# Cutting GpSimd's long elementwise operations into short ones in an attention-and-MoE kernel

## The chip, the core and the metric

The kernel runs on one core of one Trainium2 chip. The metric is the device time of one execution in microseconds (us). A core has several engines that run their own instruction streams and meet at semaphores: TensorE (PE, matmuls; its weight loads are listed as PEld), VectorE (DVE), ScalarE (ACT), GpSimd (POOL) and SyncE (SP), which here only issues DMAs. Each engine, and each DMA-issuing queue, takes its instructions in order, so an instruction that waits holds up all that stand behind it on the same engine.

## What is computed

For 8 batches, 8 heads, 576 rows and a head width of 64, a linear attention with two softmaxes is followed by a two-layer network with an exact GELU:

```python
q_s = softmax(q, over the head width)          # exp, then divided by the row's sum
k_s = softmax(k, over the sequence)
kv  = einsum('bhsd,bhse->bhde', k_s, v)        # one 64x64 matrix for each batch and head
att = einsum('bhsd,bhde->bhse', q_s, kv)       # 4608 tokens of width 512 = H*D
h   = att @ w_in                               # 512 -> 2048
out = gelu(h) @ w_out                          # 2048 -> 512, float32
```

The step that the change touches first is the division of `exp(q)` by its row sums: a multiplication of a 128x2048 bf16 tile by 32 reciprocals for each partition.

## The kernel before

The 4608 tokens are worked in chunks. Chunk c below 8 is the first 512 rows of batch c; chunk 8 collects the last 64 rows of all batches. For a chunk there are two phases: an `h` phase (`h_waves`, the first matrix product, GELU to the tile `g`) and a `y` phase (`y_phase`, the second product, into output tiles `y_sb`). Both products use Strassen-like schemes: seven block products for eight, with sums of blocks made on DVE, ACT and POOL. In the `y` phase of chunks 3 to 7 one of the seven products is itself cut a second time (class `Two`); its correction terms are put together on POOL (`corner`, `corner2`, `spread`).

While chunk c is in its `y` phase, the attention part of chunk c+1 is finished and that of batch `nb = c + 2` is begun. There is no planner: the order on every engine is written out by hand, and `after(i)` in `y_phase` runs a list of extra steps at a numbered point between the block products. For chunks 3 to 5 the steps that matter here stand in this order:

- At the head of the loop body for chunk c, `load(nb)` puts three DMAs on SP's queue: q (1 MB, line 112), k and v (1.15 MB each, line 130). On SP's queue they stand behind the two output stores of chunk c-1 (`y_store`, line 667), which end the previous `y_phase`.
- Point 8: `exp_q(nb)`, four exponentials on ACT (line 179) once q is there. Point 9: `exp_k(nb)` on ACT (line 184).
- Point 0, on POOL: `touch_g` (line 1201, a one-column operation that waits for DVE's last sum on `g`), `corner`, then the first of four casts of v to bf16 (`cast_v`, line 196). Then `corner2`, and at point 6 the other three casts.
- Point 1: `norm_q(nb)`: DVE sums the rows of `exp(q)` and takes reciprocals (lines 269 and 270), then POOL scales the tile `eq` (named `e` in the profile) in one operation of 2048 columns (line 275).
- After the fourth block product, `spread` and two additions on POOL into the output block `c22`, a 2x256 column view of a `y_sb` tile: `c22 += c12`, then `c22 -= c21` (lines 838 and 839, recorded under the helper's line 434).
- Point 5, `next_x`: on PE the attention product of chunk c+1 (line 349); on SP the DMA transpose of the scaled `eq` (line 329), which is needed one chunk later; on PE `kv_step(nb)` (line 231), 72 small matmuls of `exp(k)` with the cast v, in two halves, the first over casts 0 and 1 and the second over casts 2 and 3. On DVE stand between them `x_sums` (line 458 through the helper at 434), differences of `xT` blocks into `quad_t`, and the division of kv by its sums (lines 251 and 252).
- Then PE runs the last block product (7), and SP issues `y_store(c, 1)`, which holds `c22`, and `y_store(c, 0)`.

For c = 6 the load is `load_qrest`, eight DMAs of the remaining q rows, in place of `load(nb)`. For chunks 7 and 8 nothing is loaded. Chunk 1 also has the two additions into `c22`, with `load(4)` behind its stores.

Of the kernel before, what the change touches and what calls it, by code (L numbers as in the profile page):

```python
# [11 lines left out]
ALU = mybir.AluOpType  # L12
# [4 lines left out]
def kernel(  # L17
# [16 lines left out]
    nc = tc.nc  # L34
    B, H, S, D = q.shape
    NT, DM = out.shape
    DF = moe_w_in.shape[1]
    J = 4
# [27 lines left out]
    def bank(i, name="ps", shape=(128, 512)):  # L66
        return psum.tile(list(shape), FP32, tag=f"k{i}", name=name)
# [21 lines left out]
    HN = DM // 2  # L89
# [10 lines left out]
    def table(func):  # L100
        nc.scalar.activation(out=scr[:, 1:2], in_=scr[:, 0:1], func=func)

    st = [dict() for _ in range(B + 1)]
# [42 lines left out]
    def load(b):  # L146
        load_main(b, "q", q)
        load_pair(b, "k", k)
        load_pair(b, "v", v)

    def load_qrest():
        f = f32in.tile([128, 2048], FP32, tag="qf")
        f = f.rearrange("p (j h d) -> p j h d", j=J, h=H)
        st[B]["qf"] = f
        for b in range(B):
            nc.sync.dma_start(
                out=f[(b % 2) * R:(b % 2 + 1) * R, b // 2, :, :],
                in_=q[b, :, M:S, :].rearrange("h p d -> p h d"),
            )
# [21 lines left out]
    def exp_k(b, parts=1, part=None):  # L181
        n = HP // parts
        for i in range(0, HP, n) if part is None else (part * n,):
            nc.scalar.activation(  # L184
                out=ek[b % 2][:, i:i + n],
                in_=st[b]["kf"][:, i:i + n].rearrange("p x (n d) -> p x n d", n=NS),
                func=AF.Exp,
            )
# [75 lines left out]
    def q_sums(b, i=0, n=1):  # L264

        w = H // n
        qsum = small.tile([128, J, w], FP32, tag="qsum")
        st[b]["recq"] = small.tile([128, J, w], FP32, tag="recq", name="recq")
        nc.vector.reduce_sum(out=qsum, in_=st[b]["eq"][:, :, i * w:(i + 1) * w, :], axis=AX.X)  # L269
        nc.vector.reciprocal(st[b]["recq"], qsum)  # L270

    def q_scale(b, eng, i=0, n=1):
        w = H // n
        e = st[b]["eq"][:, :, i * w:(i + 1) * w, :]
        eng.tensor_tensor(  # L275
            out=e, in0=e, in1=st[b]["recq"].unsqueeze(3).to_broadcast([128, J, w, D]), op=ALU.mult,
        )

    def norm_q(b, i=0, n=1, eng=None):

        q_sums(b, i, n)
        q_scale(b, eng or nc.gpsimd, i, n)
# [108 lines left out]
    def s_parts(c, p0, n, which):  # L391


        g = st[c]["g"]
        a, b = slice(p0, p0 + n), slice(p0 + HK, p0 + HK + n)
        lo, hi = slice(0, HT), slice(HT, M)
        tt = nc.vector.tensor_tensor
        if 0 in which:
            tt(out=s5[:, a], in0=g[:, a, lo], in1=g[:, b, lo], op=ALU.add)
        if 1 in which:  # L400
            tt(
                out=s12[:, a].rearrange("p k (u m) -> p k u m", u=2),
                in0=g[:, a].rearrange("p k (u m) -> p k u m", u=2),
                in1=g[:, b, hi].unsqueeze(2).to_broadcast([128, n, 2, HT]), op=ALU.add,
            )
        for i, half in ((3, lo), (4, hi)):
            if i in which:
                tt(out=s12[:, a, half], in0=g[:, a, half], in1=g[:, b, hi], op=ALU.add)  # L408
        if 2 in which:
            tt(out=g[:, a, hi], in0=g[:, a, hi], in1=g[:, a, lo], op=ALU.subtract)  # L410
            tt(out=g[:, b, lo], in0=g[:, b, lo], in1=g[:, b, hi], op=ALU.subtract)  # L411
# [21 lines left out]
    def tt(out, in0, in1, op=ALU.add, eng=nc.vector):  # L433
        eng.tensor_tensor(out=out, in0=in0, in1=in1, op=op)  # L434
# [229 lines left out]
    def y_store(c, half, y_sb):  # L664
        j = 2 * half
        dst = out[c * S:c * S + M, :].rearrange("(p j) n -> p j n", j=J)[:, j:j + 2, :]
        nc.sync.dma_start(out=dst, in_=y_sb)
# [4 lines left out]
    def y_operands(c):  # L672
        g = st[c]["g"]
        act = {
            1: s12[:, :, LO], 2: s12[:, :, HI], 3: g[:, UP, LO], 4: g[:, DN, HI],
            5: s5, 6: g[:, UP, HI], 7: g[:, DN, LO],
        }
        wgt = {
            1: w16[:, 0], 2: wo_bf[:, UP, 0:HN], 3: wo_bf[:, UP, HN:DM],
            4: wo_bf[:, DN, 0:HN], 5: wo_bf[:, DN, HN:DM], 6: w16[:, 1], 7: w7,  # L680
        }
        return act, wgt
# [85 lines left out]
    def y_phase(c, ins, p3=None):  # L768

        act, wgt = y_operands(c)
        if c == 1:
            at = {"bd": 3, "be": 4, "bb": 0, "bx": 1, "ba": 2}
        else:
            at = {"bd": roles["x0"], "be": roles["x1"], "bb": roles["bb"], "bx": roles["x2"], "ba": roles["ba"]}
        bd, be, bb, bx, ba = (bank(at[n], "y" + n[1]) for n in ("bd", "be", "bb", "bx", "ba"))
        ysb = [moe_sb.tile([128, 2, DM], FP32, tag="y_sb", name="y_sb", bufs=2) for i in range(2)]
        c11, c12 = ysb[0][:, :, 0:HN], ysb[0][:, :, HN:DM]
        c21, c22 = ysb[1][:, :, 0:HN], ysb[1][:, :, HN:DM]  # L780
        f = zeros32

        def two(ps):
            return ps.rearrange("p (j n) -> p j n", j=2)

        def mm(m, ps, first):
            for j in range(2):
                for k in range(HK):
                    nc.tensor.matmul(  # L789
                        ps[:, j * HN:(j + 1) * HN], act[m][:, k, j * 128:(j + 1) * 128],  # L790
                        wgt[m][:, k, :], start=(first and k == 0 and j == 0),
                        stop=(k == HK - 1), skip_group_check=True,
                    )

        def after(i):
            for fn in ins.get(i, []):
                fn()

        if p3:
            p3.mm(c, bx, (4, 5, 1), True)  # L800
            p3.snap(bx)
        mm(4, bd, True)
        if c > 1:
            nc.scalar.copy(out=f, in_=bd)
            after(8)
            if p3:
                p3.mm(c, bx, (2, 3, 6, 7), False)
            else:
                mm(3, bx, True)
            nc.scalar.copy(out=c12, in_=two(bx))  # L810
            after(9)
        else:
            nc.vector.tensor_copy(out=f, in_=bd)
        after(0)
        if p3:
            p3.corner2(c12)
        after(6)
        mm(5, be, True)
        after(7)
        tt(f, f, be, ALU.subtract)  # L820
        after(1)
        if c > 1:
            tt(c12, c12, two(be))
        mm(1, ba, True)
        tt(c22, two(f), two(ba))
        after(2)
        mm(2, bd, False)
        nc.scalar.copy(out=c21, in_=two(bd))
        after(3)
        if c == 1:  # L830
            mm(3, be, False)
            nc.scalar.copy(out=c12, in_=two(be))
        after(10)
        mm(6, bb, True)
        tt(c22, c22, two(bb))
        if p3:
            p3.spread(c12)
        tt(c22, c22, c12, eng=nc.gpsimd)
        tt(c22, c22, c21, ALU.subtract, eng=nc.gpsimd)
        after(5)  # L840
        mm(7, ba, False)
        tt(c11, two(f), two(ba))
        y_store(c, 1, ysb[1])
        y_store(c, 0, ysb[0])
        after(4)
# [328 lines left out]
    def first_weights():  # L1174
        nonlocal y3
        y3 = Two()
        y3.weights(0)

    y_phase(1, {
        0: [sums[3]],  # L1180
        7: [lambda: norm_q(2, 0, 2)],
# [16 lines left out]
    def touch_g(c):  # L1198


        nc.gpsimd.tensor_copy(out=scr[:, 2:3], in_=st[c]["g"][:, NDF - 1, 0:1])  # L1201
# [12 lines left out]
    for c in range(2, B + 1):  # L1214
        nb = c + 2
        if 2 < c and nb < B:
            load(nb)
        elif nb == B:
            load_qrest()
        p3 = y3 if 2 < c < B else None  # L1220
        h_waves(c, q_late if c == 2 else None, p3 and p3.sums)
        s_parts(c, 4, 4, (2,))
        yi = {}
        if nb <= B:
            yi[8] = [lambda: exp_q(nb)]
            yi[1] = [lambda: norm_q(nb)]
            yi[3] = [lambda: table(AF.Gelu)]
        if nb < B:
            yi[9] = [lambda: exp_k(nb)]
            cv = [lambda hp=hp: cast_v(nb, hp, nc.gpsimd) for hp in range(HP)]  # L1230
            yi[0] = [lambda: touch_g(c)] + ([p3.corner] if p3 else []) + cv[:1]
            yi[6] = cv[1:]
        elif p3:
            yi[0] = [p3.corner]
        if c < B:
            yi[5] = [lambda: next_x(c, nb)]
            y_phase(c, yi, p3)
        else:
            y_last(c)
# [30 lines left out]
```

## Time and profile before

| what | value |
|---|---|
| median of three runs | 258.1 us (257.6 to 258.83) |
| the profiled execution: its own time | 257.78 us |
| the profiled execution: span of the trace | 255.7 us |
| PE busy | 248.8 us (97%) |
| DVE busy | 221.5 us (87%) |
| ACT busy | 190.9 us (75%) |
| POOL busy | 89.8 us (35%), 100 instructions |
| granted clock of TensorE | 1.00 |

The page lists busy time by engine, then groups of instructions by source line, with the operands by the program's names, the shape (partitions x columns) and how often they ran. In the lists in order of time, the first column is the start in us from the start of the span, the second the duration; a bracket at the end gives idle time of the engine ahead of the instruction and what ended it. "x4" after a shape means that four such instructions in a row are told as one line.

### The profile page before, as it was taken

What the parts mean: (1) busy time and instruction counts of PE and PEld (TensorE: products, weight loads), DVE (VectorE), ACT (ScalarE), POOL (GpSimd) and SP (SyncE); (2) the same over time, 40 slices, a digit from 0 to 9 for tenths busy, and PEclk for the clock granted to TensorE, in tenths of its full rate; (3) what the DMA queues carried; (4) which work ended last, traced back from release to release, by engine and by line L of the source; (5) the groups of instructions that cost most, each with busy time, mean ns of one, the idle gap of its engine ahead of it and who ended that gap; (6) DMA issues with size and microseconds to landing.
All of it is one profiled execution on the core that took longest, in us unless ns stands there. A gap on an engine that the chain in (4) does not pass through costs nothing.

```text
span 255.7 us, 6732 instructions
## 1 busy us (share of the span) xinstructions
PE 248.8 (97%) x2732; PEld 195.7 (77%) x2738; DVE 221.5 (87%) x395; ACT 190.9 (75%) x326; POOL 89.8 (35%) x100
## 2 busy tenths in 40 slices
PE   7999999999999999999999999999999999999994
PEld 3444444448888889898889878987899889988883
DVE  1878799888986999998999899989999999878972
ACT  4785988699977995889588968896787778258711
POOL 1530023001949377007900691059203920540000
PEclk9999999999999999999999999999999999999999
DMA  7999999994549925980379137922760250013033
GB/s 241 400 368 425 401 406 399 399 411 171 75 145 326 276 47 145 328 315 1 85 252 402 49 71 231 385 98 47 224 146 3 46 200 2 3 44 124 0 82 85
DMA packets 43167, 50.23 MB, mean 196 GB/s; under 512 B 20225, under 2 KB 30465, under 8 KB 42881
## 3 DMA queue, kind: packets, MB, share of 16 engines
q1 hardware_dynamic: 42416, 49.13, 56.6%
q10 hardware_dynamic: 720, 0.69, 1.1%
q8 instruction: 21, 0.34, 0.5%
q14 instruction: 10, 0.07, 0.1%
HBM read 36.70 MB, written 9.44 MB: 180 GB/s over the span
## 4 chain that ended last, share of the span: by engine, by line
PE 83%; DVE 6%; DMA 4%; ACT 2%; issue 2%; ACTq 0%; POOL 0%; DVEq 0%
PE qa L503 19%; PE ps L383 11%; PE qb L503 10%; PE yd L789 8%; PE ya L789 7%; PE ps L648 5%; PE qc L503 4%; PE ye L789 4%; PE yb L789 3%; PE yx L743 2%; DMA f<-in_v_dram 2%; DMA touch<-in_moe_w_in_dram 2%; DVE qsum L269 2%; DVE y_sb L434 2%; PE kv L231 1%
## 5 line engine op out<-in xcount | busy, mean ns | idle before, releaser
L503 PEld LDWEIGHTS <-quad_s 128*128 128x128 bf16 x448 | 43.4, 98 | 7.7 <-DVE kvc L252 1.1
L275 POOL TENSOR_TENSOR e<-e,recq 128x2048 bf16<-128x2048 bf16 (+1 forms) x9 | 27.4, 3046 | 49.7 <-DVE recq L270 49.1
L789 PEld LDWEIGHTS <-g 128*128 128x128 bf16 x368 | 35.2, 98 | 4.8 <-issue 0.4
L503 PEld LDWEIGHTS <-wi_bf 128*128 128x128 bf16 x336 | 32.8, 98 | 3.9
L789 PEld LDWEIGHTS <-s 128*128 128x128 bf16 x336 | 32.7, 98 | 3.7
L503 PE MATMUL qa<-quad_t,quad_s 128*128 128x256 bf16 x224 | 29.8, 272 | 0.2 <-DVE qb L434 0.2
L383 PE MATMUL ps<-xT,wi_bf 128*128 128x512 bf16 x124 | 27.8, 379 | 0.3
L269 DVE TENSOR_REDUCE qsum<-e 128x16 f32<-128x1024 bf16 (+1 forms) x12 | 20.9, 1745 | 6.8 <-ACT e L179 6.6
L383 PEld LDWEIGHTS <-wi_bf 128*128 128x128 bf16 x128 | 12.4, 98 | 15.2 <-issue 0.6
L527 ACT ACTIVATE g<-r 128x512 bf16<-128x512 f32 x28 | 17.3, 631 | 7.3 <-DVE r L434 7.3
L511 ACT COPY qc<-qa 128x512 f32<-128x512 f32 x26 | 13.9, 577 | 11.4 <-PE qa L503 5.6
L389 ACT ACTIVATE g<-ps 128x512 bf16<-128x512 f32 x32 | 17.6, 603 | 6.2 <-PE ps L383 5.8
L434 DVE TENSOR_TENSOR qb<-qa,r 128x512 f32<-128x512 f32 x28 | 18.1, 691 | 4.6 <-ACT g L527 2.9
L179 ACT ACTIVATE e<-f 128x512 bf16<-128x512 f32 (+1 forms) x42 | 20.5, 556 | 2.0 <-DMA f<-in_q_dram 1.8
L527 ACT ACTIVATE g<-qc 128x512 bf16<-128x512 f32 x28 | 15.2, 594 | 8.2 <-PE qc L503 8.2
L434 POOL TENSOR_TENSOR y_sb<-y_sb 128x512 f32<-128x512 f32 x14 | 18.9, 1351 | 3.7 <-issue 2.8
L408 DVE TENSOR_TENSOR s<-g 128x1024 bf16<-128x1024 bf16 x28 | 19.8, 726 | 0.0
L196 POOL CAST v_aug<-f 128x576 bf16<-128x576 f32 x25 | 17.4, 723 | 3.7 <-DMA f<-in_v_dram 3.5
L434 DVE TENSOR_TENSOR r<-qa,r 128x512 f32<-128x512 f32 x28 | 17.9, 680 | 0.8 <-PE qa L503 0.7
L1201 POOL CAST scr<-g 128x1 f32<-128x1 bf16 x4 | 0.7, 187 | 49.5 <-DVE g L411 49.5
L184 ACT ACTIVATE ek<-f 128x2304 bf16<-128x2304 f32 (+1 forms) x10 | 17.4, 1735 | 0.5 <-DMA f<-in_k_dram 0.5
L503 PE MATMUL qb<-quad_t,quad_s 128*128 128x256 bf16 x112 | 15.6, 273 | 0.3 <-DVE kvc L252 0.2
(116 smaller groups left out, 536.7 us busy)
## 6 DMA issues: line engine op xcount, KB each, us to landing
out_dram<-y_sb SPq DMA_DIRECT2D x16, 512.0 KB, 4.3
f<-in_k_dram SPq DMA_DIRECT2D x6, 1152.0 KB, 9.9
f<-in_v_dram SPq DMA_DIRECT2D x6, 1152.0 KB, 11.6
f<-in_q_dram SPq DMA_DIRECT2D x6, 1024.0 KB, 8.2
w<-in_moe_w_in_dram SPq DMA_DIRECT2D x6, 512.0 KB, 9.1
f<-in_v_dram SPq DMA_DIRECT2D x8, 288.0 KB, 6.3
f<-in_q_dram SPq DMA_DIRECT2D x4, 512.0 KB, 8.9
w<-in_moe_w_out_dram SPq DMA_DIRECT2D x2, 1024.0 KB, 12.3
```

The lines of the kernel that those rows point to most:

```text
L179: nc.scalar.activation(out=dst[:, i], in_=src[:, u], func=AF.Exp)
L184: nc.scalar.activation(out=ek[b % 2][:, i:i + n], in_=st[b]["kf"][:, i:i + n].rearrange("p x (n d) -> p x n d", n=NS), func=AF.Exp,)
L196: eng.tensor_copy(out=o, in_=i)
L269: nc.vector.reduce_sum(out=qsum, in_=st[b]["eq"][:, :, i * w:(i + 1) * w, :], axis=AX.X)
L275: eng.tensor_tensor(out=e, in0=e, in1=st[b]["recq"].unsqueeze(3).to_broadcast([128, J, w, D]), op=ALU.mult,)
L383: nc.tensor.matmul(ps, wi_bf[:, dm, t * 128:(t + 1) * 128], st[c]["xT"][:, dm, :], start=(dm == 0), stop=(dm == NDM - 1),)
L389: nc.scalar.activation(out=st[c]["g"][:, t, :], in_=ps, func=AF.Gelu)
L408: tt(out=s12[:, a, half], in0=g[:, a, half], in1=g[:, b, hi], op=ALU.add)
L434: eng.tensor_tensor(out=out, in0=in0, in1=in1, op=op)
L503: nc.tensor.matmul(held[kind, q][:, u], w, mov[m][:, k], start=(m in (1, 5) and u == 0 and k == 0), stop=(k == 1), skip_group_check=True,)
L527: nc.scalar.activation(out=g[:, t:t + 2, half], in_=held[kind, q], func=AF.Gelu)
L789: nc.tensor.matmul(ps[:, j * HN:(j + 1) * HN], act[m][:, k, j * 128:(j + 1) * 128], wgt[m][:, k, :], start=(first and k == 0 and j == 0), ...
```

## The change

The scaling of `eq` by POOL at point 1, in chunks 2 to 6, becomes eight operations of 256 columns, each over four heads of one of the four row groups. The row sums and reciprocals on DVE stay one operation each. The scalings of batches 0 to 3 stay as they are.

The two additions into `c22`, in all of chunks 1 to 7, become eight operations of 128 columns: first the four parts of `c22 += c12`, then the four parts of `c22 -= c21`. The arithmetic on each element is the same.

```diff
+    def q_scale_parts(b):
+
+        for j in range(J):
+            for i in (0, 4):
+                e = st[b]["eq"][:, j, i:i + 4, :]
+                nc.gpsimd.tensor_tensor(
+                    out=e, in0=e, op=ALU.mult,
+                    in1=st[b]["recq"][:, j, i:i + 4].unsqueeze(2).to_broadcast([128, 4, D]),
+                )
...
         if p3:
             p3.spread(c12)
-        tt(c22, c22, c12, eng=nc.gpsimd)
-        tt(c22, c22, c21, ALU.subtract, eng=nc.gpsimd)
+        for x, op in ((c12, ALU.add), (c21, ALU.subtract)):
+            for j in range(2):
+                for n in (slice(0, 128), slice(128, HN)):
+                    tt(c22[:, j, n], c22[:, j, n], x[:, j, n], op, eng=nc.gpsimd)
         after(5)
...
             yi[8] = [lambda: exp_q(nb)]
-            yi[1] = [lambda: norm_q(nb)]
+            yi[1] = [lambda: q_sums(nb), lambda: q_scale_parts(nb)]
             yi[3] = [lambda: table(AF.Gelu)]
```

## The prediction

> **What bounds the kernel now.** I read the page first, then the chain of work that ended last, then each engine's list in order of time around one `y` phase (chunk 4, 137 to 160 us), and last the DMA issues with their time to landing.
>
> The page, with the groups that the change touches:
>
> ```profile
> PE 248.8 (97%) x2732; PEld 195.7 (77%) x2738; DVE 221.5 (87%) x395; ACT 190.9 (75%) x326; POOL 89.8 (35%) x100
> ...
> L275 POOL TENSOR_TENSOR e<-e,recq 128x2048 bf16<-128x2048 bf16 (+1 forms) x9 | 27.4, 3046 | 49.7 <-DVE recq L270 49.1
> ...
> L434 POOL TENSOR_TENSOR y_sb<-y_sb 128x512 f32<-128x512 f32 x14 | 18.9, 1351 | 3.7 <-issue 2.8
> ```
>
> PE is the bound on the whole, and POOL seems to have two thirds of the span to spare. But the average hides a tight ring. POOL's list for chunk 4:
>
> ```profile
> 142.43 0.19 POOL L1201 CAST scr<-g 128x1 f32<-128x1 bf16 x1 [14.06 <-DVE g L411]
> 142.57 0.99 POOL L434 TENSOR_TENSOR two_d<-two_d 128x128 f32<-128x128 f32 x2
> 143.59 0.66 POOL L196 CAST v_aug<-f 128x576 bf16<-128x576 f32 x1
> 144.21 0.99 POOL L434 TENSOR_TENSOR two_d<-two_d,y_sb 128x128 f32<-128x128 f32 x2
> 145.15 1.88 POOL L196 CAST v_aug<-f 128x576 bf16<-128x576 f32 x3
> 146.99 3.62 POOL L275 TENSOR_TENSOR e<-e,recq 128x2048 bf16<-128x2048 bf16 x1
> 150.57 1.05 POOL L434 TENSOR_TENSOR y_sb<-y_sb,two_d 128x128 f32<-128x128 f32 x2
> 151.69 2.88 POOL L434 TENSOR_TENSOR y_sb<-y_sb 128x512 f32<-128x512 f32 x2
> ```
>
> From 142.43 to 154.57 POOL has no gap. What it ends with releases SP's queue, here for chunks 3 and 4:
>
> ```profile
> 128.39 0.84 SPq L667 DMA_DIRECT2D out_dram<-y_sb  x2
> ...
> 132.13 0.66 SPq L130 DMA_DIRECT2D f<-in_v_dram  x1
> ...
> 154.60 0.84 SPq L667 DMA_DIRECT2D out_dram<-y_sb  x2
> ...
> 157.87 0.73 SPq L130 DMA_DIRECT2D f<-in_v_dram  x1
> ```
>
> The store goes out 0.03 us after POOL's last addition (151.69 + 2.88 = 154.57), and the next batch's q, k and v stand behind it. The issues between 129 and 134 us, with time to landing in the last column:
>
> ```profile
> f<-in_v_dram SPq DMA_DIRECT2D x1, 1152.0 KB, 11.3
> ```
>
> So v lands at 132.13 + 11.3 = 143.4, and POOL's first cast of it starts at 143.59, just behind `corner` (142.57 + 0.99 = 143.56). Here v arrives just when it is wanted. For chunk 5 it lands at 157.87 + 11.5 = 169.4, and the cast starts at 169.71. The casts end at 147.03, and PE asks for them soon after:
>
> ```profile
> 147.66 0.81 PE L231 MATMUL kv<-v_aug,ek 64*64 64x65 bf16 x72
> ```
>
> Its second half, at about 148.0, needs the last two casts: 0.95 us to spare. The ring is v landing, casts, scaling, additions, store, loads, v landing: 143.4 to 169.4, 26.0 us, while PE takes 150.16 - 124.25 = 25.9 and 26.2 us for these two chunks. POOL is thus almost a second bound in chunks 3 to 5.
>
> The other thing to see is a DVE operation on the chain:
>
> ```profile
> 149.24 1.65 DVE quad_t L434
> ...
> 151.35 1.05 PE qb L503 x8
> ```
>
> This difference of two SBUF blocks takes 0.41 us elsewhere. Here it ends at 150.89, 0.28 after POOL's scaling ended at 150.61. In chunks 3 and 5 it is the same (1.56 and 1.57 us, ending 0.29 and 0.28 after the scaling). DVE is shut out until POOL's long operation is over, and PE's next product starts late.
>
> **What the change takes away.** DVE's wait shrinks from up to the rest of a 3.62 us operation to at most the rest of a short one. Its worth on PE is read from PE's starts, where eight such matmuls take 0.87 us: the product behind starts 0.19, 0.32 and 0.25 us late in chunks 3, 4, 5, the one that waits on `e_sum` behind the third `quad_t` another 0.13, 0.12, 0.12, and 0.37 in chunk 6; chunks 2 and 7 lose nothing. That is 1.5 us at most. [...]
>
> **What it adds on POOL.** The scaling took 3.62 us for 2048 columns and 1.90 for 1024, so 0.185 us is fixed and a part of 256 columns costs 0.185 + 0.43 = 0.61. Independent POOL operations overlap a little (three casts of 0.66 take 1.88, a spacing of 0.61), so eight parts take 7 x 0.57 + 0.61 = 4.6 us: +1.0. For the additions the nearest row is exact in shape: 128x128 float32 takes 0.455 alone. At a spacing of 0.41 eight take 3.3, at the 0.50 of the pair `two_d` (dependent, 0.99 for two) 4.0; two long ones take 2.62 where DVE leaves them alone (chunk 1). I take 3.4, nearer the independent spacing, since each subtraction depends on an addition four places ahead: +0.8. [...]
>
> Each DVE operation that now gets in holds POOL: the first `spread` operation took 0.63 against 0.455, the first addition 1.46 against 1.27, so 0.2 each. In the scaling that is one or two `quad_t` differences, and since POOL runs later into the next chunk, the fourth one and the three sums of `Two.sums` (156.09 to 157.0) meet it too: 3 to 5 more, +0.7. Together POOL ends 2.5 us later in a chunk. Low end 1.5 (0.9, 0.6, nothing for DVE), high end 3.6 (1.3, 1.3, 1.0).
>
> **What waits behind it.** SP's transpose waits for the last part, 1.3 us or more later; its result is wanted 25 us later, nothing. The stores and loads move by the full 2.5.
> - Chunk 1: only the additions, +0.8; v for chunk 2 lands at 77.11 + 12.2 = 89.3, wanted at 90.96. Hidden. Chunk 7's store has no load behind it, nothing.
> - Chunk 2: about +2.2 (no `spread`); v lands at 103.75 + 11.3 = 115.05, wanted at 117.39. Just hidden; without that cover it would add to all that follows.
> - Chunk 3's lateness meets chunk 4: v late by 2.5, less 0.95: kv, and PE behind it, 1.55 us late.
> - Chunk 4's ring starts from that late v and adds 2.5: 2 x 2.5 less 0.95 less the 0.3 by which v was early: PE 3.7 us late against before.
> - Chunk 5 adds 2.5 again; behind its store stand the eight loads of the remaining q. The last is issued at 187.6 and lands 3.2 later at 190.8; its exponential starts at 193.63, 2.8 to spare. From it DVE's row sums run without a gap to the last `xT` copy, ready 0.2 before PE's product at 201.85. So 3 x 2.5 - 0.3 - 2.8 - 0.2 = 4.2 us late, which includes the 3.7.
> Lateness counted from a landing swallows what PE gained ahead of it, so of the 1.5 only chunk 6's 0.3 is left: +3.9.
>
> The q and k loads are covered: in chunk 4 q lands at 129.28 + 8.4 = 137.7 for 141.30, k at 140.6 for 143.87.
>
> **Sum.** The profiled execution took 257.78 us (span 255.7, 2.1 around it), 0.3 under the median of 258.1. 257.8 + 3.9 = 261.7, and 262.0 on the median's scale. With 1.5 us a chunk, chunk 5 decides: 2 x 1.5 - 1.25 - 0.3 = +1.4, 259.5; with 3.6: 10.8 - 3.3 - 0.3 = +7.2, 265.3.
>
> **Rivals.**
> - The relief wins (faster). The place is the first `quad_t` difference behind the attention product, the price 1.5 us on PE, less what is left of a short wait (0.3 us of some 1.2): 257.0. It needs POOL's added time to stay below about 0.85 us a chunk, since 2 x 0.85 - 1.25 - 0.3 is near zero. For it: the wait stands on the chain three times. Against it: 14 more instructions with a fixed 0.185 less 0.05 overlap make 1.8 already. [...] Chance 0.10.
> - The lateness is hidden: v is there earlier than the landing time says, or the ring has a microsecond more in it. Then only the relief and DVE's new short waits are left, and they cancel: 258.1. Against it: the cast of chunk 4 starts 0.03 after its forerunner, where unhindered casts start 0.04 before its end. Chance 0.08.
> - Worse than the ring: short POOL operations shut DVE out again and again (14 openings of 0.2 to 0.5 us in DVE's fullest stretch), and the lateness of chunk 2 joins in. By the ring 4 x 2.5 - 2.3 - 3.3 = +4.4, and half a microsecond of DVE's lateness in each of four chunks adds 2: +6.4, 264.5 and more. Chance 0.10.
>
> **How the numbers follow.** My forecast has 0.72. The measurement tells about 0.5% (1.3 us) from no change. Slower is the forecast and the worse case, 0.72 + 0.10 = 0.82; same 0.08; faster 0.10. The range from 259.0 to 265.5 runs from the low cost, half a microsecond under it for a partial relief, to the high cost; it leaves out the relief, the hidden case and the far end of the worst.
>
> **What would show it.** POOL's scaling as eight of about 0.6 us spanning 4.6 to 5.2, the additions as eight of 0.45 to 0.6 spanning 3.3 to 4.2; the first `quad_t` difference down from 1.6 to 0.5 to 1.0 us; the stores of chunk 3 at about 131 and of chunk 4 some 5 later than before; POOL idle ahead of line 196 until `f<-in_v_dram`; PE waiting ahead of line 231 for `v_aug` in chunks 4 and 5, and the exponential of chunk 6 waiting for `f<-in_q_dram`. I am wrong if the store of chunk 3 moves by less than 1 us, or if casts wait for v and PE does not wait for casts.

## The result, and the profile after

The changed kernel is slower: 261.42 us median (261.02 to 262.39) against 258.17, a ratio of 1.013 (95% interval 1.009 to 1.017). A second series on another occasion gave 261.85 against 257.85, 1.015 (1.014 to 1.017). The profiled execution took 261.10 us with a span of 259.0.

The page after, first the totals, then the two groups of the change (the added function moves line 434 to 444):

```profile
PE 250.9 (97%) x2738; PEld 197.5 (76%) x2738; DVE 219.3 (85%) x395; ACT 190.8 (74%) x326; POOL 103.5 (40%) x177
...
L444 POOL TENSOR_TENSOR y_sb<-y_sb 128x128 f32<-128x128 f32 x56 | 26.1, 500 | 2.8 <-issue 2.8
L284 POOL TENSOR_TENSOR e<-e,recq 128x256 bf16<-128x256 bf16 x40 | 24.9, 657 | 1.8 <-DVE recq L270 1.2
```

DVE's busy time fell by 2.2 us, as it waits less inside its operations (the mean of `quad_t<-xT` is 579 ns and was 951). POOL's rose by 13.7. That POOL is busy for 40% of the span and idle for the rest says nothing about the loss. POOL's list in order of time around chunk 4, and the first cast of chunk 5, does:

```profile
145.42 0.66 POOL L196 CAST v_aug<-f 128x576 bf16<-128x576 f32 x1 [2.30 <-DMA f<-in_v_dram]
146.04 0.98 POOL L444 TENSOR_TENSOR two_d<-two_d,y_sb 128x128 f32<-128x128 f32 x2
146.97 1.88 POOL L196 CAST v_aug<-f 128x576 bf16<-128x576 f32 x3
148.82 5.15 POOL L284 TENSOR_TENSOR e<-e,recq 128x256 bf16<-128x256 bf16 x8
153.93 0.86 POOL L444 TENSOR_TENSOR y_sb<-y_sb,two_d 128x128 f32<-128x128 f32 x2
154.76 4.01 POOL L444 TENSOR_TENSOR y_sb<-y_sb 128x128 f32<-128x128 f32 x8
...
173.37 0.66 POOL L196 CAST v_aug<-f 128x576 bf16<-128x576 f32 x1 [3.17 <-DMA f<-in_v_dram]
```

The scaling takes 5.15 us in place of 3.62, the additions 4.01 in place of 2.88. POOL now stands idle for 2.30 and 3.17 us ahead of the first cast because v is not there; before, it had no gap at that place. The reason stands on SP's queue, chunks 3 and 4:

```profile
130.51 0.83 SPq L677 DMA_DIRECT2D out_dram<-y_sb  x2
...
133.78 0.79 SPq L130 DMA_DIRECT2D f<-in_v_dram  x1
...
158.79 0.83 SPq L677 DMA_DIRECT2D out_dram<-y_sb  x2
...
162.05 0.83 SPq L130 DMA_DIRECT2D f<-in_v_dram  x1
```

The store of chunk 3 goes out 2.12 us later than before (130.51 against 128.39), that of chunk 4 4.19 later (158.79 against 154.60): the lateness adds up around the ring. The chain of work that ended last shows how it reaches PE in chunk 4:

```profile
133.78 11.52 DMA f<-in_v_dram
...
146.04 0.45 POOL two_d L444
...
147.06 0.70 DVE y_sb L444
...
147.80 0.67 PE ps L359 x7
148.47 0.40 DVE y_sb L444
...
148.91 0.47 PE kv L231 x34
```

In the chain of before, this stretch was PE's matmuls up to 139 us and then ACT and DVE work, with no DMA in it. Now it is the transfer of v, `corner2` on POOL (which stands behind the first cast), DVE's addition into `c12` (which has to wait for `corner2` to have read it: DVE idles 1.40 us until then), PE's attention product (one of its output banks is the one that this addition empties: PE idles 0.64 us until then), and the second half of kv.

What held that second half back is not the DVE row that the chain names. DVE's list has it as

```profile
148.45 0.69 DVE L444 TENSOR_TENSOR y_sb<-y_sb,yb 128x512 f32<-128x512 f32 x1
```

and so running on to 149.14, while the second half starts at 148.91. What had just ended is POOL's last cast (146.97 + 1.88 = 148.85), and in the trace the matmul at 148.91 waits on the semaphore that POOL's casts raise. So two branches lead from the late v to PE: a first wait through `corner2` and DVE, and behind it a last one for the casts. The product behind kv waits for both, and it is the last that counts.

### The profile page after: what moved, and what is told of

The parts are those of the page before. It is cut to its first block, busy times and chain, and to the rows that moved or that the text cites. A ratio compares the mean times of both kernels' runs of the same rounds, so it can differ in the third digit from the quotient of the medians.

```text
span 259.0 us, 6822 instructions
## 1 busy us (share of the span) xinstructions
PE 250.9 (97%) x2738; PEld 197.5 (76%) x2738; DVE 219.3 (85%) x395; ACT 190.8 (74%) x326; POOL 103.5 (40%) x177
## 4 chain that ended last, share of the span: by engine, by line
PE 77%; DMA 13%; DVE 4%; SPq 2%; issue 2%; POOL 1%; POOLq 0%; DVEq 0%
PE qa L513 15%; DMA f<-in_v_dram 11%; PE ps L393 11%; PE ya L799 9%; PE qb L513 7%; PE yd L799 7%; PE ps L658 5%; PE ye L799 4%; PE qc L513 4%; PE yb L799 3%; PE kv L231 2%; PE yx L753 2%; PE ps L359 2%; DMA f<-in_q_dram 2%; PE ya L882 1%
## 5 line engine op out<-in xcount | busy, mean ns | idle before, releaser
L799 PEld LDWEIGHTS <-g 128*128 128x128 bf16 x368 | 36.0, 100 | 5.5 <-issue 0.4
L513 PE MATMUL qa<-quad_t,quad_s 128*128 128x256 bf16 x224 | 29.2, 273 | 0.0
L275 POOL TENSOR_TENSOR e<-e,recq 128x1024 bf16<-128x1024 bf16 (+1 forms) x4 | 9.3, 2330 | 48.1 <-DVE recq L270 48.1
L444 POOL TENSOR_TENSOR y_sb<-y_sb 128x128 f32<-128x128 f32 x56 | 26.1, 500 | 2.8 <-issue 2.8
L284 POOL TENSOR_TENSOR e<-e,recq 128x256 bf16<-128x256 bf16 x40 | 24.9, 657 | 1.8 <-DVE recq L270 1.2
```

The lines of the kernel that those rows point to most:

```text
L284: nc.gpsimd.tensor_tensor(out=e, in0=e, op=ALU.mult, in1=st[b]["recq"][:, j, i:i + 4].unsqueeze(2).to_broadcast([128, 4, D]),)
L513: nc.tensor.matmul(held[kind, q][:, u], w, mov[m][:, k], start=(m in (1, 5) and u == 0 and k == 0), stop=(k == 1), skip_group_check=True,)
L799: nc.tensor.matmul(ps[:, j * HN:(j + 1) * HN], act[m][:, k, j * 128:(j + 1) * 128], wgt[m][:, k, :], start=(first and k == 0 and j == 0), ...
```

## The experiments

**The changed kernel once more** (no edit).

> The changed kernel once more, for a second trace. It is to show whether the stretch of product 7 in chunk 5 that took 3.50 us instead of 1.75 for sixteen matmuls (granted clock 0.97 over that chunk) belongs to the change or to that one execution. Ring theory (POOL's added 2 us a chunk delay the stores, the loads behind them, the casts of v and PE): 261 to 262 us with or without the slow stretch, and POOL idle ahead of the first cast of v by 1.5 to 2.5 us in chunk 4 and by 2.5 to 4 in chunk 5. Rival (the throttled clock makes up half of the loss): an execution at clock 1.00 takes 259.5 us or less.

Measured: 261.85 us, ratio 1.015 (1.014 to 1.017). The trace is of an execution at clock 1.00, and its product 7 in chunk 5 takes the usual 1.75 us; yet its time is that of the series. POOL waits 2.95 us (above the 1.5 to 2.5 that I gave) and 3.20 us for v. What it loses in place of the slow stretch shows in ACT's list for chunk 6, where the exponential's table load waits for the last of the remaining q rows:

```profile
196.86 1.28 ACT L179 ACT_TABLE_LOAD   x1 [1.42 <-DMA f<-in_q_dram]
```

The other executions say the same: six of the nine of the changed kernel have a mean clock of 0.993, about what one such stretch makes (3.41 us at 0.50 in a span of 259.0), and none of the 17 of the kernel before in the second series is under 0.998. Those six average 261.7 us, the three at 1.00 average 261.5. So the throttled stretch is not what costs the time; the rival falls. A lateness that is counted from a landing swallows a loss on PE ahead of it, as it swallows a gain.

**Each half alone.** In the first kernel the additions are whole again:

```diff
-        for x, op in ((c12, ALU.add), (c21, ALU.subtract)):
-            for j in range(2):
-                for n in (slice(0, 128), slice(128, HN)):
-                    tt(c22[:, j, n], c22[:, j, n], x[:, j, n], op, eng=nc.gpsimd)
+        tt(c22, c22, c12, eng=nc.gpsimd)
+        tt(c22, c22, c21, ALU.subtract, eng=nc.gpsimd)
```

> The scaling in eight parts, the additions whole. Ring theory: POOL ends 1.2 to 1.4 us later a chunk (the scaling spans 4.8 to 5.0 us against 3.62), which the 0.95 us of chunk 4 and the 1.25 us of chunks 4 and 5 together mostly cover; PE is late by 0.3 in chunk 4 and 1.2 in chunk 5, less 0.5 to 0.8 of relief: 258.0 to 259.3 us. Rival (short POOL operations as such disturb DVE, in proportion to their number, 40 of the 96 new ones): about 0.4 of the whole loss, 259.5 us.

Measured: 259.36 us (258.39 to 260.25), ratio 1.006 (1.004 to 1.008), just above the range of the ring and nearer to the rival's 259.5. POOL waits 1.85 us for v in chunk 4 and 1.81 in chunk 5.

In the second the scaling is whole and the additions are split:

```diff
-            yi[1] = [lambda: q_sums(nb), lambda: q_scale_parts(nb)]
+            yi[1] = [lambda: norm_q(nb)]
```

> The additions in eight parts, the scaling whole. Ring theory: POOL ends 0.8 to 0.9 us later a chunk, less than chunk 4's slack of 0.95, so the casts are hardly late and the first quad_t difference still waits out the scaling (1.6 us): 257.8 to 258.8 us. The two halves of the change together then lose far less than the whole change, since each alone stays about inside the slack. Rival (disturbance in proportion to the number of operations, 56 of 96): 0.6 of the loss, 260.1 us.

Measured: 258.43 us (257.52 to 259.83), ratio 1.003 (1.001 to 1.004). In chunk 4 the cast finds v in time, in chunk 5 POOL waits 1.06 us. The two halves cost 0.6% and 0.3%, both together 1.5%. The disturbance in proportion to the number of operations would have split 1.5% into 0.6 and 0.9; the larger number of operations gave the smaller loss. Neither figure decides alone between the theories, but a sum of 0.9% against 1.5% is what slack that is used up looks like.

**The loads taken out of the ring.** The changed kernel, with the next batch's loads on SP's queue ahead of the transpose and the output stores:

```diff
-        if 2 < c and nb < B:
-            load(nb)
-        elif nb == B:
-            load_qrest()
...
-            yi[5] = [lambda: next_x(c, nb)]
+            ahead = []
+            if nb + 1 < B:
+                ahead = [lambda: load(nb + 1)]
+            elif nb + 1 == B:
+                ahead = [load_qrest]
+            yi[5] = ahead + [lambda: next_x(c, nb)]
```

> The change as it is, but the loads of the batch after next are put on SP's queue at point 5, ahead of the transpose and the output stores, so nothing that is loaded waits for POOL's additions. Ring theory: the casts of v never wait, the loss goes and the relief of DVE remains: 256.4 to 257.5 us, faster than the kernel before, with the quad_t difference at 0.5 to 0.8 us. Rival (short operations themselves cost the time, by shutting DVE out or by POOL's own length): still 261 us.

Measured: 255.53 us (255.47 to 256.12), ratio 0.992 (0.991 to 0.993): faster than both kernels, and 0.9 us below the range that I gave. The short operations are all still there with nearly the same lengths (in chunk 4 the scaling takes 4.97 us against 5.15, the additions 3.71 against 4.01), and the casts of chunks 3 to 5 never wait:

```profile
142.91 0.66 POOL L196 CAST v_aug<-f 128x576 bf16<-128x576 f32 x1
143.54 0.99 POOL L444 TENSOR_TENSOR two_d<-two_d,y_sb 128x128 f32<-128x128 f32 x2
144.47 1.88 POOL L196 CAST v_aug<-f 128x576 bf16<-128x576 f32 x3
146.31 4.97 POOL L284 TENSOR_TENSOR e<-e,recq 128x256 bf16<-128x256 bf16 x8
```

The rival, that short operations as such cost the time, falls. The first `quad_t` difference in DVE's list of the same chunk:

```profile
148.65 0.84 DVE L444 TENSOR_TENSOR quad_t<-xT 128x512 bf16<-128x512 bf16 x1
```

0.84 us against 1.65 before.

**The same loads in the kernel before** (the same edit on whole operations).

> The kernel before (scaling and additions whole) with the loads put ahead of the transpose at point 5. Ring theory with relief: before, the ring just fitted, so loading early alone brings little, 257.3 to 258.0 us, and the first quad_t difference still waits out the scaling at about 1.6 us in chunks 3 to 5; what the split kernel gained with early loads (255.5) is then DVE's relief, some 2 us. Rival (the early loads themselves are the gain, the split is neutral): 255.5 us here too.

Measured: 257.46 us (257.17 to 258.10), ratio 0.999 (0.998 to 1.000). The `quad_t` difference still waits out the scaling:

```profile
149.18 1.56 DVE L434 TENSOR_TENSOR quad_t<-xT 128x512 bf16<-128x512 bf16 x1
```

With the loads where they were, the split costs 1.5%; with the loads early, it brings 0.8% against whole operations' 0.1%. The split's relief of DVE is real, about 1.8 us (0.7% by the ratios; 1.9 by the medians of two occasions, 257.46 and 255.53); in the changed kernel the ring takes it back.

**Early loads, scaling split, additions whole** (the two edits above together).

> Early loads, the scaling in eight parts, the additions whole. Ring theory: with no load behind them the additions' length is of no account; what they do to DVE is. If the relief is that of the scaling, 255.5 to 256.2 us; if the parts of the additions bring half of it (DVE's third quad_t difference no longer waits up to 1.3 us), 256.2 to 256.8. Rival (short additions disturb DVE): 255.0 us or less, faster than with both.

Measured: 255.66 us (255.40 to 255.91), ratio 0.991 (0.990 to 0.992), the same as with both splits within the intervals. The relief is that of the scaling; the split of the additions brings nothing that these series can tell.

**Delay without splitting.** The kernel before with eight memsets of a scratch tile on POOL behind the scaling:

```diff
+    pad = singles.tile([128, 256], BF16)
...
-            yi[1] = [lambda: norm_q(nb)]
+            yi[1] = [lambda: norm_q(nb)] + [lambda: nc.gpsimd.memset(pad, 0.0)] * 8
```

> The kernel before with eight small memsets of a scratch tile on POOL behind the scaling at point 1 in chunks 2 to 6: nothing is split, POOL is only kept busy for about 2 us longer ahead of the output additions, with operations that read nothing. Ring theory: the stores and loads are late by that, the casts of v wait 1.5 to 3.5 us in chunks 4 and 5, and the time is that of the changed kernel or a little more, 260.5 to 263 us, since the relief is missing too. Rival (the number of short operations that read what DVE reads): within 0.5 us of before.

Measured: 264.01 us (263.23 to 264.96), ratio 1.024 (1.022 to 1.026), above the range I gave. Two reasons are in POOL's and DVE's lists of chunk 4:

```profile
146.57 0.66 POOL L197 CAST v_aug<-f 128x576 bf16<-128x576 f32 x1 [2.21 <-DMA f<-in_v_dram]
...
149.97 3.62 POOL L276 TENSOR_TENSOR e<-e,recq 128x2048 bf16<-128x2048 bf16 x1
153.52 2.89 POOL L1227 MEMSET pad<- 128x256 bf16 x8
```

```profile
151.40 2.46 DVE L435 TENSOR_TENSOR quad_t<-xT 128x512 bf16<-128x512 bf16 x1
...
154.59 0.41 DVE L435 TENSOR_TENSOR quad_t<-xT,quad_t 128x512 bf16<-128x512 bf16 x1
```

The memsets took 2.89 us, not 2; and the scaling, late itself, now shuts DVE's first difference out for 2.46 us instead of 1.65. Nothing is split here, and the casts of v wait as in the changed kernel. POOL's time ahead of the store is enough to make a loss.

**The first cast behind corner2.** In the changed kernel:

```diff
-            yi[0] = [lambda: touch_g(c)] + ([p3.corner] if p3 else []) + cv[:1]
-            yi[6] = cv[1:]
+            yi[0] = [lambda: touch_g(c)] + ([p3.corner] if p3 else [])
+            yi[6] = cv
```

> The changed kernel with the first cast of v put behind corner2 on POOL, so that corner2, which does not need v, no longer stands behind a wait for v. In the changed kernel DVE's addition into c12 waits for corner2, and PE's attention product for DVE. If that route carries the loss, PE's attention product starts on time and only the second half of the kv products waits for the last casts: 259 to 260.5 us. If the casts in front of kv carry it, as the prediction had it, the time stays: 261 to 262 us.

Measured: 260.22 us (259.52 to 261.44), ratio 1.009 (1.007 to 1.011), between the kernel before and the changed one. PE's list of chunk 4:

```profile
147.18 0.63 PE L359 MATMUL ps<-qT,kvc 64*64 64x512 bf16 x8
147.63 0.53 PE L231 MATMUL kv<-v_aug,ek 64*64 64x65 bf16 x38
148.55 0.47 PE L231 MATMUL kv<-v_aug,ek 64*64 64x65 bf16 x34 [0.39 <-POOL v_aug L196]
```

The attention product is on time, and only the second half of kv waits, for the casts, by 0.39 us. The time is in the range that I gave for `corner2`, but the run does not tell the two routes apart, because the edit also brings the casts together:

```profile
146.01 2.49 POOL L196 CAST v_aug<-f 128x576 bf16<-128x576 f32 x4 [1.04 <-DMA f<-in_v_dram]
```

From the first cast's start to the last one's end it is 2.49 us now and was 3.43 in the changed kernel (145.42 to 148.85), where `corner2` stood between them. So the last cast ends 0.9 us sooner behind v whichever route carries the loss; I had overlooked that. The traces do tell them apart. In chunks 4 and 5 the last cast ends later than before by 1.82 and 3.65 us in the first trace of the changed kernel, 2.76 and 4.61 in the second, 1.47 and 2.57 here; the product behind kv starts later by 0.91 and 2.66, 1.85 and 3.63, 0.56 and 1.58. It is the casts' lateness less 0.9 to 1.0 in all six, with and without the wait through `corner2`. In these chunks that wait is real and hidden behind the casts; what `corner2` costs is the 0.9 us by which it holds up the last three of them. The exponential of chunk 6 waits for its q rows here too (1.15 us).

## Why the prediction was right

The forecast was 262.0 us, +3.9, with 259.0 to 265.5; measured were 261.4 and 261.9, +3.3 and +4.0. Point by point:

- *The ring.* Right in place and mechanism. Loading early takes the loss away with all short operations in place; delaying POOL without splitting makes one. One number beside it mixed two views: the 25.9 us of PE for chunk 4 took its start from the chain (124.25) and its end from the list (150.16). From list to list it is 26.1 (124.09 to 150.16); against a ring of 26.0 there is still next to no room.
- *POOL's prices.* The scaling was to span 4.6 to 5.2 us and spans 4.79 to 5.16; the additions 3.3 to 4.2 and span 3.53 to 4.02. The fixed 0.185 us for an operation, from the 1024 and 2048 column rows, carried over: the median part of the scaling takes 0.612 us, and 0.61 was forecast.
- *The sum on POOL a chunk.* 2.5 forecast. From the first cast to the store it was 11.00 us in chunk 3 before (117.39 to 128.39) and 13.10 after (117.41 to 130.51), +2.1; in chunks 4 and 5 +2.4 (145.42 to 158.79) and +1.9 (173.37 to 186.26); in the second trace +2.1, +2.4 and +2.4. If the 1.8 for the parts themselves stands, the term that was too high is the 0.7 for DVE's operations that get in: 0.1 to 0.6 is left for it.
- *Chunk 1 and chunk 2 hidden.* Right in the first trace: the stores were 0.80 and 1.92 us later (0.8 and 2.2 forecast), and chunk 3's first cast started at 117.41 against 117.39. In the second trace the cover was not quite enough: v held up the first cast of chunk 2 by 0.33 us, and that of chunk 3 started at 117.86, 0.47 late, behind a v that by my estimate landed at 117.7 (the cast's start less the 0.12 us between landing and cast in chunk 4 of the first trace).
- *The way from v to PE.* Right: the casts hold up the second half of kv, with the spare of 0.95 us (0.9 to 1.0 measured, see the last experiment). What it left out is the earlier wait, of the attention product through `corner2`; I had named `corner2` in the ring and not asked who waits for it. That cost nothing here, since the wait for the casts ended later. The forecast for chunk 4 was 1.55 us late; in the two traces the product behind kv started 0.91 and 1.85 late (149.31 and 150.25 against 148.40). The second is above the forecast although POOL's sum a chunk was below it, since chunk 2's 0.47 came on top and this v took an estimated 12.0 us to land (146.36 less 0.12 less its issue at 134.26) instead of 11.3; that the two roughly cancel over the whole is chance.
- *Chunk 5.* 3.7 forecast; the product behind kv came 2.66 and 3.63 us late (177.26 and 178.23 against 174.60).
- *Chunk 6.* 4.2 forecast; the next h phase started 3.77 and 4.13 us late (205.62 and 205.98 against 201.85). In the second trace the exponential waits for q, as forecast. In the first it does not: some 1.6 us came from the throttled stretch told below (by the chain, product 7 took 3.50 us there and 1.85 in chunk 4). That the ends agree there is partly chance.
- *The relief.* The gain on PE was sized at 1.5 us at most; the early loads show 1.8 to 1.9. With them the h phases behind chunks 3 to 7 start 0.13, 0.60, 1.15, 1.64 and 2.14 us earlier than before, 0.5 for each of the last four, where I had counted 0.32 to 0.44. I had read only the starts of the groups of eight matmuls and missed what PE loses inside one: the eight behind `e_sum` span 1.19 us before, where the others span 1.04, so some 0.15 us more in each of these chunks.
- *The rivals.* The relief that wins needed less than 0.85 us of added POOL time a chunk; it was 2.1. It did win where the ring was opened. Nothing was hidden by an early v. DVE was not shut out again and again: the mean of `quad_t<-xT` fell from 951 to 579 ns, while `quad_t<-xT,quad_t` rose from 501 to 564 and the two kinds of sums of `Two.sums` from 411 to 463 and from 280 to 358.

## What to carry to other kernels

An engine that is idle for most of the span can still close a ring (POOL was busy for 35% of it before): follow its last operation to what it releases (here a store, and the loads queued behind it) and add up one turn against the period of the loop. Cutting GpSimd's operation of 3.62 us into eight let VectorE in here (its first difference in chunk 4 took 0.84 us with early loads, against 1.65 before), at a fixed price of 0.185 us an operation (the eight span 4.79 to 5.16 us); pay such a price only where nothing that matters is queued behind, or move that queue first. Of a step that gets late, ask for every reader and every writer of what it touches, also those that only wait for it to have read; then ask which of these waits ends last, since only that one costs time.

## What the runs showed of the hardware

**A throttled stretch after a short wait.** In the first trace of the changed kernel, PE waited 0.29 and 1.17 us in chunk 5, ran the small kv products, and then took 3.50 us for sixteen matmuls that take 1.85 in chunk 4. The table by stretches (busy time by engine, then the granted clock):

```profile
core 0: us, PE busy (x) PEld busy (x) DVE busy (x) ACT busy (x) POOL busy (x), PEclk, DMA share, GB/s
...
175.70:177.30 1.60, 1.41 (x80) 1.18 (x80) 1.50 (x3) 1.07 (x2) 1.60 (x3) 0.99 0.04 10
177.30:180.80 3.50, 3.50 (x21) 2.49 (x19) 2.75 (x8) 0.00 (x0) 3.50 (x7) 0.52 0.00 0
180.80:183.00 2.20, 2.20 (x23) 1.97 (x21) 1.14 (x2) 1.65 (x4) 2.20 (x5) 1.00 0.01 3
```

The clock is 0.52 over these 3.5 us (0.50 from 177.26 to 180.67, 3.41 us) and then full again (1.00 from 180.80 to 183.00). In the second trace nearly the same waits (0.35 and 1.15) left it at 1.00. In the 3.41 us ahead of the stretch (173.85 to 177.26) PE was busy for 1.81 us, with little but the attention product and the small kv products; no run here shows what set the clock back in the one trace and not in the other.

**Who shuts whom out.** DVE's difference of two SBUF blocks was held by POOL's scaling, which reads SBUF, to its end (2.46 us, from 151.40 to 153.86 in the delayed kernel; the scaling ended at 153.59), but ran in 0.41 and 0.42 us in the middle of the memsets, which read nothing (154.59 and 155.52, between 153.52 and 156.41). Whether the reading decides it, or something else in which the two differ, no run here shows.
